# An attention-and-FFN kernel on one core: image lines issued ahead of the queries, key weights on the scalar queue, a third of the first tile's output products an iteration earlier

## The chip, the core and the metric

One NeuronCore of a Trainium2 chip, alone on the chip. The metric is device time of one execution in microseconds; lower is better. Times are medians of single runs, each 1.9 us or so longer than the span from the first to the last instruction that a profile shows. "Before" is the kernel before the change, "the changed kernel" the one after. Faster or slower needs two per cent, which is 21 us here. The "clock" is TensorE's, as a share of full speed.

## The reference, cut to what matters

```python
# q: 4 x 12288 x 128, kv: 4 x 384 x 32 x 128 (an image), w_sr: 128 x 128
kv_pool = kv.reshape(B, H // 4, 4, W // 4, 4, C).mean(axis=(2, 4))   # 4 x 4 pixels to one: 768 keys
k = v = kv_pool.reshape(B, -1, C) @ w_sr
a = softmax(q @ k.T / sqrt(C));  x = a @ v                            # 4 x 12288 rows of 128
gate = maximum(x @ w_gate, 0);   val = x @ w_val                      # 128 -> 1536
return (gate * val) @ w_out                                           # 1536 -> 128
```

## The kernel before

The 49152 rows are 96 tiles of 512. The main loop runs over k. In iteration k TensorE takes, interleaved in twelve steps, the scores of tile k, the attention values of tile k-1, the gate and value products of tile k-3 and the output products of tile k-4. ScalarE does the exponentials and the casts of the value products, VectorE multiplies gate by value. All products go through eight PSUM banks, which every function takes from one pool (`bank`). Before the loop comes a start in which the keys of the first image are made while it is still being loaded: pair 0 (four image lines of 512 KB each, `dh` 0 to 3), then pairs 1 and 2. "The eighth image line" is the last one of pair 1.

```python
    w_sr_f32 = const.tile([128, C], FP32)
    nc.sync.dma_start(w_sr_f32, w_sr)              # key weights, 64 KB
    q_load_plain(0, 1)                             # queries of tile 0: 256 KB in rows of 2 KB
    kv_load(0, 0)                                  # four image lines, 512 KB each, rows of 4 KB
    q_load_plain(1, GRP)                           # queries of tiles 1 to 3: 768 KB
    for pair in range(1, NJC // 2):
        kv_load(0, pair)
...
    idle = bank([128, 128])
    for _ in range(34):                            # warm-up products
        nc.tensor.matmul(idle, ident16, ident16, start=True, stop=True)
...
    q_cast(0)                                      # VectorE: queries to 16 bits
    q_turn_pe(0)                                   # TensorE: transposed, VectorE: copied
    turn_open(0, 0)
    for dh in range(r):                            # TensorE: transposes that add up the lines
        turn_add(0, 0, line(0, dh), first=dh == 0, final=dh == r - 1)
    q_cast(1)
    project(0, 0)
...
    for k in range(LAG, last + 1):                 # LAG = 3; iteration 3 is the first
        ...
        for step in range(NFB):                    # twelve steps
            kO, kF = k - LAG - 1, k - LAG
            if 0 <= kO:
                out_proj(kO, step)                 # four products of 128 columns
                ...
            if kF < NT:
                value_proj(kF, step)               # TensorE 512 columns, ScalarE cast
            if k == LAG:                           # attention values left over from the start
                own, left = left[:2], left[2:]
                for kV, jc, half in own:
                    values(kV, jc, half)
                    if jc == NJC - 1:
                        keep_sums(kV, half)                  # VectorE: reciprocal
                        keep_values(kV, half, nc.scalar)     # ScalarE: two scalings by it
                        if half == 1:
                            x_turn(kV)
            elif step % 2 == 0:
                if k < NT:
                    scores(k, step // 2)           # TensorE 512 columns, ScalarE exponential
            elif k > GRP and k - 1 < NT:           # not in iteration 4
                values(k - 1, 2 * i, half)
                values(k - 1, 2 * i + 1, half)
                ...
            if kF < NT:
                gate_proj(kF, step)                # TensorE 512 columns, VectorE gate * value
```

The softmax here doesn't subtract the row's maximum and nothing guards it: scores larger than these inputs give would overflow.

Of the kernel before, what the change touches and what calls it, by code (L numbers as in the profile page):

```python
# [9 lines left out]
FP32 = mybir.dt.float32  # L10
FP16 = mybir.dt.float16
AF = mybir.ActivationFunctionType
# [4 lines left out]
def kernel(  # L17
# [22 lines left out]
    nc = tc.nc  # L40
# [8 lines left out]
    NFB = D_FF // 128  # L49
# [6 lines left out]
    LAG = GRP - 1  # L56
# [6 lines left out]
    const = ctx.enter_context(tc.tile_pool(name="const", bufs=1))  # L63
# [3 lines left out]
    def bank(shape, dtype=FP32):  # L67
        return psum.tile(shape, dtype, tag="bank", name="bank_ps")
# [4 lines left out]
    def q_load(g):  # L73
        if not 0 <= g < NG:
            return
        b, n0 = divmod(g * GRP * T, N)
        q16 = work.tile([128, GRP * NS, C], FP16, tag="q16", bufs=2)
        nc.gpsimd.dma_start(  # L78
            q16, q[b, n0 : n0 + GRP * T, :].rearrange("(p s) c -> p s c", p=128)
        )  # L80
        q16s[g] = q16

    def q_turn(g):
        if not 0 <= g < NG:
            return
        q16 = q16s.pop(g)
        qT = work.tile([128, GRP * NS, 128], FP16, tag="qT", bufs=3)
        nc.sync.dma_start_transpose(qT, q16.rearrange("p s c -> p (s c)"))
        qTs[g] = qT

    def q_load_plain(i0, i1):
        q32 = work.tile([128, i1 - i0, NS, C], FP32, tag=f"q32_{i0}", bufs=1, name="q32")
        nc.sync.dma_start(  # L93
            q32, q[0, 0 : GRP * T, :].rearrange("(p i s) c -> p i s c", p=128, i=GRP)[:, i0:i1]
        )
        for i in range(i0, i1):
            q32s[i] = q32[:, i - i0]

    def q_cast(i):
        q16 = work.tile([128, NS, C], FP16, tag="q16s", bufs=3, name="q16s")  # L100
        nc.vector.tensor_copy(q16, q32s[i])
        q16s[0, i] = q16

    def q_turn_pe(i):
        q16 = q16s.pop((0, i))
        qt_ps = bank([128, NS, 128], FP16)
        for s in range(NS):
            nc.tensor.transpose(qt_ps[:, s, :], q16[:, s, :], ident16)
        if i == 0:
            qTs[0] = work.tile([128, GRP * NS, 128], FP16, tag="qT", bufs=3, name="qT")  # L110
        nc.vector.tensor_copy(qTs[0][:, i * NS : (i + 1) * NS, :], qt_ps)
# [7 lines left out]
    kv16 = const.tile([128, B, NJC, 2 * C + 4], FP16)  # L119
    kv_in = {}  # L120

    def kv_load(b, pair):
        parts = work.tile([128, r, 2, r, C], FP32, tag="kv_in", bufs=3)
        rows = kv[b, pair * 2 * HC : (pair + 1) * 2 * HC].rearrange(
            "(hp dh) (wp h dw) c -> dh hp wp (h dw c)", dh=r, h=2, dw=r
        )
        for dh in range(r):
            nc.sync.dma_start(parts[:, dh].rearrange("p h dw c -> p (h dw c)"), rows[dh])  # L128
        kv_in[b, pair] = parts

    s3s, kv_Ts, key_banks = {}, {}, {}
# [14 lines left out]
    def turn_open(b, pair):  # L146
        kv_Ts[b, pair] = bank([128, 2, 128])

    def turn_add(b, pair, lines, first=False, final=False, chunks=(0, 1)):

        n = lines.shape[2]
        for h in chunks:
            for i in range(n):
                nc.tensor.matmul(  # L154
                    kv_Ts[b, pair][:, h], lines[:, h, i], ident, is_transpose=True,
                    start=(first and h == i == 0), stop=(final and i == n - 1),
                    skip_group_check=True,
                )
        if final and h == 1:
            kvT = work.tile([128, 2, 128], FP32, tag="kvT", bufs=2)  # L160
            nc.vector.tensor_copy(kvT, kv_Ts[b, pair])  # L161
            kv_Ts[b, pair] = kvT

    def project(b, pair):
        pr = bank([128, 2, 128])
        nc.tensor.matmul(pr, w_sr_f32, kv_Ts.pop((b, pair)), start=True, stop=True)  # L166
        nc.vector.tensor_scalar(  # L167
            kv16[:, b, 2 * pair : 2 * pair + 2, 0:C], pr, 1.0 / (r * r), None, op0=ALU.mult
        )
# [32 lines left out]
    def keep_sums(k, half):  # L202
        rinvs[k, half] = work.tile([128, 2, 1], FP32, tag="rinv", bufs=4, name="rinv")
        nc.vector.reciprocal(rinvs[k, half], x_banks[k, half][:, :, C : C + 1])  # L204
# [49 lines left out]
    def out_add(k, fb, s, o_ps, first):  # L254
        nc.tensor.matmul(  # L255
            o_ps, hTs[k][:, fb, s * 128 : (s + 1) * 128], wo16[:, fb, :],
            start=first, stop=(fb == NFB - 1), skip_group_check=True,
        )

    def out_proj(k, fb):  # L260
        if fb == 0:
            o_banks[k] = bank([128, NS, 128])
        for s in range(NS):
            out_add(k, fb, s, o_banks[k][:, s, :], fb == 0 and s == 0)

    def out_scale(k, engine, own, o_ps=None):
        if k not in o_sbs:
            o_sbs[k] = work.tile([128, NS, 128], FP32, tag="o_sb", bufs=3, name="o_sb")
        o_sb, o_ps = o_sbs[k][:, own], o_ps if o_ps is not None else o_banks[k]
        if engine is nc.scalar:  # L270
            nc.scalar.mul(o_sb, o_ps, 1.0 / X_SCALE**2)
        else:
            nc.vector.tensor_scalar(o_sb, o_ps, 1.0 / X_SCALE**2, None, op0=ALU.mult)  # L273
# [28 lines left out]
    ctx.enter_context(tc.manual_schedule())  # L302


    warm = const.tile([128, 1], FP32)
    nc.vector.memset(warm, 0.0)
    nc.scalar.activation(warm, warm, AF.Exp)
    ident = const.tile([128, 128], FP32)
    make_identity(nc, ident)
    ident16 = const.tile([128, 128], FP16)  # L310
# [1 line left out]
    nc.gpsimd.memset(kv16[:, :, :, 2 * C : 2 * C + 4], 1.0 / X_SCALE)  # L312

    w_sr_f32 = const.tile([128, C], FP32)
    nc.sync.dma_start(w_sr_f32, w_sr)
    q_load_plain(0, 1)
    kv_load(0, 0)
    q_load_plain(1, GRP)
    for pair in range(1, NJC // 2):
        kv_load(0, pair)  # L320

    wg16 = const.tile([128, D_FF], FP16)
    wv16 = const.tile([128, D_FF], FP16)
# [12 lines left out]
    def line(pair, dh):  # L336
        return kv_in[0, pair][:, dh]
# [9 lines left out]

    s2s = {}
    q_cast(0)
    q_turn_pe(0)  # L350
    turn_open(0, 0)
    for dh in range(r):
        turn_add(0, 0, line(0, dh), first=dh == 0, final=dh == r - 1)
    q_cast(1)
    project(0, 0)
    q_cast(2)
# [68 lines left out]
    for k in range(LAG, last + 1):  # L425
        g, ph = divmod(k, GRP)
        if ph == 1:
            q_turn(g + 1)
            q_load(g + 2)
        b = k // NST + 1  # L430
        at = k % NST - (NST - NJC - 6)
        for step in range(NFB):
            kO, kF = k - LAG - 1, k - LAG
            half, i = divmod(step // 2, NJC // 2)
            if 0 <= kO:
                out_proj(kO, step)
                if step == NFB - 1 and k < last:
                    out_scale(kO, nc.vector if kF < NT - 2 else nc.scalar, slice(0, NS))
                    out_store(kO, slice(0, NS))
            if kF < NT:  # L440
                value_proj(kF, step)
            if k == LAG:
# [4 lines that stand above are left out]
                        keep_sums(kV, half)  # L447
                        keep_values(kV, half, nc.scalar)
# [4 lines that stand above are left out]
                    scores(k, step // 2)  # L453
            elif k > GRP and k - 1 < NT:
                values(k - 1, 2 * i, half)
                values(k - 1, 2 * i + 1, half)
                if i == NJC // 2 - 1:
                    keep_sums(k - 1, half)
                    keep_values(k - 1, half)
                    if half == 1:  # L460
                        x_turn(k - 1)
            if kF < NT:
                gate_proj(kF, step)
            if k == LAG and step == 2:
                x_turn_pe(1)
            if b < B:
                if step == 1 and 0 <= at < NJC and at % 2 == 0:
                    kv_load(b, at // 2)
                if step == 3 and 0 <= at - 2 < NJC:
                    pool_pixels(nc.gpsimd, b, (at - 2) // 2, at % 2)  # L470
                pair = (at - 5) // 2
                if at % 2 == 1 and 0 <= pair < NJC // 2:
                    if step == 2:
                        turn_open(b, pair)
                        turn_add(b, pair, s3s.pop((b, pair))[:, :, None], True, True)
                    if step == 4:
                        project(b, pair)
                    if step == 8:
                        turn_values(b, pair)
# [33 lines left out]
```

## Time and profile before

| | before |
|---|---|
| median, first three runs | 1047.56 us (1047.43 to 1047.84) |
| span of the profile | 1046.1 us |
| busy TensorE / VectorE / ScalarE | 99 / 87 / 87 % |
| first value product of iteration 3 | 32.46 us |
| second scores product of iteration 5 | 52.98 us |

The last two rows are marks in the trace. The first says how long the start took. The second lies in the part where TensorE runs without a gap, and from there to the end the kernel takes 993 us or so. What lies between the two, 20.52 us, is the stretch of iterations 3 and 4 with the beginning of 5, and it tells of the output products apart from the loads. The profile's lines for before are in the prediction.

### The profile page before, as it was taken

Reading aid. Unit: us, or ns where it says so; the run is one execution under the profiler, and the core shown is the slowest. Engines: PE = TensorE matmul, PEld = TensorE weight load, DVE = VectorE, ACT = ScalarE, POOL = GpSimd, SP = SyncE. Lnnn points to the kernel's source line nnn. Section 1 sums busy time; section 2 is a strip of 40 time slices with the busy share of each in tenths; the row PEclk is TensorE's granted clock in tenths of the full one; section 3 lists DMA queues with packets and bytes.
Section 4 is the critical chain, followed back from the end, with each engine's and each line's share of the span. In section 5 each row is a group of like instructions: output and inputs, shape, how many; then the busy total and the mean of one; then the engine's idle time right before and its main releaser. Section 6 shows DMA issues by size and latency. Waiting matters only on the chain.

```text
span 1046.1 us, 25977 instructions
## 1 busy us (share of the span) xinstructions
PE 1036.3 (99%) x9984; PEld 691.0 (66%) x9984; DVE 913.6 (87%) x1679; ACT 908.6 (87%) x1741; POOL 107.6 (10%) x127
## 2 busy tenths in 40 slices
PE   8999999999999999999999999999999999999998
PEld 6566666666666666666666666666666666666665
DVE  3788889898888888998888888889988888888898
ACT  3888888888888888888888888888888888888887
POOL 2000045200000015500000003430000000000000
PEclk9999999999999999999999999999999999999999
DMA  8733256241322335523224144551332322212111
GB/s 298 123 81 72 73 186 164 55 87 32 86 52 65 74 122 139 156 60 72 56 63 87 31 87 132 148 151 41 77 62 56 72 64 55 67 32 67 32 47 47
DMA packets 125853, 90.75 MB, mean 87 GB/s; under 512 B 103328, under 2 KB 104224, under 8 KB 125728
## 3 DMA queue, kind: packets, MB, share of 16 engines
q1 hardware_dynamic: 120288, 75.85, 26.9%
q0 software_dynamic: 5440, 13.24, 7.7%
q8 instruction: 78, 1.28, 0.5%
q14 instruction: 47, 0.39, 0.1%
HBM read 52.76 MB, written 25.17 MB: 74 GB/s over the span
## 4 chain that ended last, share of the span: by engine, by line
PE 97%; DMA 1%; SPq 1%; DVE 1%; ACT 0%; issue 0%; DVEq 0%; ACTq 0%
PE bank_ps L255 25%; PE bank_ps L234 24%; PE bank_ps L245 24%; PE bank_ps L196 12%; PE bank_ps L185 12%; DMA parts<-in_kv_dram 1%; PE bank_ps L154 1%; PE bank_ps L166 1%; SPq L128 0%; ACT aT L186 0%; ACT x L210 0%; ACT val L238 0%; SPq L93 0%; PE bank_ps L174 0%; DVE hT L248 0%
## 5 line engine op out<-in xcount | busy, mean ns | idle before, releaser
L248 DVE SCALAR_TENSOR_TENSOR hT<-bank_ps,val 128x512 f16<-128x512 f32 x1152 | 759.6, 687 | 100.7 <-ACT val L238 74.8
L238 ACT CAST val<-bank_ps 128x512 f16<-128x512 f32 x1152 | 677.8, 591 | 112.1 <-PE bank_ps L234 107.8
L255 PEld LDWEIGHTS <-hT 128*128 128x128 f16 x4608 | 351.4, 98 | 199.9 <-issue 0.4
L255 PE MATMUL bank_ps<-wo,hT 128*128 128x128 f16 x4608 | 443.6, 219 | 0.0
L234 PE MATMUL bank_ps<-xT,wv 128*128 128x512 f16 x1152 | 437.1, 379 | 0.1
L245 PE MATMUL bank_ps<-xT,wg 128*128 128x512 f16 x1152 | 436.1, 379 | 0.1
L186 ACT ACTIVATE aT<-bank_ps 128x512 f16<-128x512 f32 x576 | 346.4, 605 | 17.9 <-PE bank_ps L185 17.5
L196 PE MATMUL bank_ps<-kv,aT 128*128 128x129 f16 x2304 | 223.4, 220 | 0.0
L196 PEld LDWEIGHTS <-aT 128*128 128x128 f16 x2304 | 177.2, 98 | 68.3 <-issue 0.4
L185 PE MATMUL bank_ps<-qT,kv 128*128 128x512 f16 x576 | 216.6, 379 | 1.5 <-DVE kv L167 0.8
L245 PEld LDWEIGHTS <-wg 128*128 128x128 f16 x1152 | 111.5, 97 | 66.1 <-issue 1.0
L234 PEld LDWEIGHTS <-wv 128*128 128x128 f16 x1152 | 112.7, 98 | 0.5 <-issue 0.4
L212 DVE TENSOR_TENSOR x<-bank_ps,rinv 128x256 f16<-128x256 f32 x188 | 79.7, 424 | 6.7 <-DVE rinv L204 0.2
L78 POOL DMA_DIRECT2D q<-in_q_dram x23 | 12.5, 543 | 569.7 <-DMA qT<-q 569.5
L273 DVE TENSOR_SCALAR o_sb<-bank_ps 128x512 f32<-128x512 f32 (+1 forms) x95 | 64.0, 674 | 1.3 <-PE bank_ps L255 1.3
L137 POOL TENSOR_TENSOR s<-parts 128x512 f32<-128x512 f32 x36 | 45.2, 1267 | 163.9 <-DMA parts<-in_kv_dram 122.4
L185 PEld LDWEIGHTS <-kv 128*128 128x128 f16 x576 | 55.8, 98 | 2.5 <-DVE kv L167 1.6
L204 DVE RECIPROCAL rinv<-bank_ps 128x2 f32<-128x2 f32 x192 | 30.7, 160 | 1.6 <-PE bank_ps L196 1.6
L139 POOL TENSOR_TENSOR s<-s 128x512 f32<-128x512 f32 x18 | 22.8, 1268 | 1.4
L141 POOL TENSOR_TENSOR c<-s 128x256 f32<-128x256 f32 x18 | 13.0, 725 | 1.4
L161 DVE COPY kvT<-bank_ps 128x256 f32<-128x256 f32 x12 | 5.0, 417 | 7.8 <-PE bank_ps L154 7.8
L144 POOL TENSOR_TENSOR kv_s<-c 128x128 f32<-128x128 f32 x18 | 8.2, 454 | 1.4
(37 smaller groups left out, 82.5 us busy)
## 6 DMA issues: line engine op xcount, KB each, us to landing
parts<-in_kv_dram SPq DMA_DIRECT2D x48, 512.0 KB, 6.1
out_dram<-o_sb SPq DMA_DIRECT2D x95, 256.0 KB, 2.1
q<-in_q_dram POOLq DMA_DIRECT2D x23, 512.0 KB, 5.3
xT<-x SPq DMA_TRANSPOSE x94, 2.5
q<-in_q_dram SPq DMA_DIRECT2D x1, 768.0 KB, 8.5
wv<-in_moe_w_val_dram POOLq DMA_DIRECT2D x2, 192.0 KB, 4.4
wg<-in_moe_w_gate_dram POOLq DMA_DIRECT2D x2, 192.0 KB, 4.8
wo<-in_moe_w_out_dram POOLq DMA_DIRECT2D x1, 384.0 KB, 9.6
```

The costliest lines, as they stand in the source:

```text
L137: eng.tensor_tensor(s2[:, i], parts[:, 2 * i, h], parts[:, 2 * i + 1, h], op=ALU.add)
L185: nc.tensor.matmul(s_ps, kv16[:, k // NST, jc, 0:C], qT_of(k), start=True, stop=True)
L186: nc.scalar.activation(aTs[k][:, jc, :], s_ps, AF.Exp, scale=qk_scale)
L196: nc.tensor.matmul(x_ps[:, i, :], aTs[k][:, jc, s * 128 : (s + 1) * 128], kv16[:, k // NST, jc, C : 2 * C + 1], start=(jc == 0 and i == 0) ...
L204: nc.vector.reciprocal(rinvs[k, half], x_banks[k, half][:, :, C : C + 1])
L212: nc.vector.tensor_tensor(x16s[k][:, 2 * half : 2 * half + 2, :], x_ps[:, :, 0:C], rinv.to_broadcast([128, 2, C]), op=ALU.mult,)
L234: nc.tensor.matmul(va_ps, wv16[:, fb * 128 : (fb + 1) * 128], xTs[k], start=True, stop=True)
L238: nc.scalar.copy(val, va_ps)
L245: nc.tensor.matmul(g_ps, wg16[:, fb * 128 : (fb + 1) * 128], xTs[k], start=True, stop=True)
L248: nc.vector.scalar_tensor_tensor(hTs[k][:, fb, :], g_ps, 0.0, vals.pop((k, fb)), op0=ALU.max, op1=ALU.mult)
L255: nc.tensor.matmul(o_ps, hTs[k][:, fb, s * 128 : (s + 1) * 128], wo16[:, fb, :], start=first, stop=(fb == NFB - 1), skip_group_check=True,)
L273: nc.vector.tensor_scalar(o_sb, o_ps, 1.0 / X_SCALE**2, None, op0=ALU.mult)
```

## The change

The intent, not yet a finding: image lines reach the chip earlier, because nothing stands ahead of them in SyncE's queue; the array's clock comes up earlier, because the first transposes follow the warm-ups at once; and TensorE fills its stalls at the end of iteration 3 with work that iteration 4 would have to do.

```diff
--- before.py
+++ after.py
@@ -119,13 +119,15 @@
     kv16 = const.tile([128, B, NJC, 2 * C + 4], FP16)
     kv_in = {}
 
-    def kv_load(b, pair):
+    def kv_load(b, pair, between=None):
         parts = work.tile([128, r, 2, r, C], FP32, tag="kv_in", bufs=3)
         rows = kv[b, pair * 2 * HC : (pair + 1) * 2 * HC].rearrange(
             "(hp dh) (wp h dw) c -> dh hp wp (h dw c)", dh=r, h=2, dw=r
         )
         for dh in range(r):
             nc.sync.dma_start(parts[:, dh].rearrange("p h dw c -> p (h dw c)"), rows[dh])
+            if dh == 1 and between is not None:
+                between()
         kv_in[b, pair] = parts
 
     s3s, kv_Ts, key_banks = {}, {}, {}
@@ -302,9 +304,6 @@
     ctx.enter_context(tc.manual_schedule())
 
 
-    warm = const.tile([128, 1], FP32)
-    nc.vector.memset(warm, 0.0)
-    nc.scalar.activation(warm, warm, AF.Exp)
     ident = const.tile([128, 128], FP32)
     make_identity(nc, ident)
     ident16 = const.tile([128, 128], FP16)
@@ -312,12 +311,15 @@
     nc.gpsimd.memset(kv16[:, :, :, 2 * C : 2 * C + 4], 1.0 / X_SCALE)
 
     w_sr_f32 = const.tile([128, C], FP32)
-    nc.sync.dma_start(w_sr_f32, w_sr)
-    q_load_plain(0, 1)
-    kv_load(0, 0)
+    nc.scalar.dma_start(w_sr_f32, w_sr)
+    kv_load(0, 0, between=lambda: q_load_plain(0, 1))
     q_load_plain(1, GRP)
     for pair in range(1, NJC // 2):
         kv_load(0, pair)
+
+    warm = const.tile([128, 1], FP32)
+    nc.vector.memset(warm, 0.0)
+    nc.scalar.activation(warm, warm, AF.Exp)
 
     wg16 = const.tile([128, D_FF], FP16)
     wv16 = const.tile([128, D_FF], FP16)
@@ -347,10 +349,11 @@
 
     s2s = {}
     q_cast(0)
-    q_turn_pe(0)
     turn_open(0, 0)
     for dh in range(r):
         turn_add(0, 0, line(0, dh), first=dh == 0, final=dh == r - 1)
+        if dh == 1:
+            q_turn_pe(0)
     q_cast(1)
     project(0, 0)
     q_cast(2)
@@ -432,8 +435,13 @@
         for step in range(NFB):
             kO, kF = k - LAG - 1, k - LAG
             half, i = divmod(step // 2, NJC // 2)
+            if k == LAG and step >= NFB - 4:
+                out_proj(kF, step - NFB + 4)
+            if k == LAG + 1 and step % 3 > 0:
+                out_proj(kO, 4 + step - 1 - step // 3)
             if 0 <= kO:
-                out_proj(kO, step)
+                if kO > 0:
+                    out_proj(kO, step)
                 if step == NFB - 1 and k < last:
                     out_scale(kO, nc.vector if kF < NT - 2 else nc.scalar, slice(0, NS))
                     out_store(kO, slice(0, NS))
```

## The prediction

> **What bounds the kernel now.** I read the page's first part, then its chain of work that ended last.
>
> ```profile
> PE 1036.3 (99%) x9984; PEld 691.0 (66%) x9984; DVE 913.6 (87%) x1679; ACT 908.6 (87%) x1741; POOL 107.6 (10%) x127
> PE 97%; DMA 1%; SPq 1%; DVE 1%; ACT 0%; issue 0%; DVEq 0%; ACTq 0%
> ```
>
> A busy PE may only be a pipelined one, so the second line decides: 97% of the chain is TensorE's own work. In order of time, the chain is one unbroken row of matmuls from 43 us to the end. So there is no gain in the body; whatever moves the moment at which TensorE runs without gaps moves the end by as much. The change touches only what lies before 52 us. I therefore read that stretch closely, first the chain in order of time (start, length, what):
>
> ```profile
> 0.74 0.40 SPq L315
> 1.20 0.42 SPq L93
> 1.67 0.65 SPq L128
> ...
> 7.02 10.92 DMA parts<-in_kv_dram
> 18.04 0.70 DVE kv_s L343
> ```
>
> The end hangs on the landing at 17.94 us of the eighth image line (the last of pair 1). The waits of pair 0 and of the first query are not on the chain. The lines ahead of it are SyncE's issues: the key weights, the first queries, then image lines. How fast bytes come in is told by the table of stretches (us; then busy time per engine, clock, DMA share, GB/s):
>
> ```profile
> 0.00:2.00 2.00, 0.28 (x3) 0.29 (x4) 0.06 (x1) 1.27 (x1) 1.11 (x8) 1.00 0.04 13
> 2.00:3.00 1.00, 1.00 (x13) 1.00 (x11) 0.00 (x0) 0.22 (x2) 0.00 (x0) 1.00 0.64 156
> 3.00:4.00 1.00, 1.00 (x12) 1.00 (x11) 0.00 (x0) 0.00 (x0) 0.00 (x0) 1.00 0.79 127
> 4.00:5.00 1.00, 1.00 (x13) 1.00 (x11) 0.07 (x1) 0.00 (x0) 0.00 (x0) 1.00 0.76 309
> 13.00:20.00 7.00, 6.02 (x51) 3.87 (x51) 4.97 (x11) 4.04 (x8) 0.00 (x0) 1.00 1.03 414
> ```
>
> From 13 us the queue is full at 414 GB/s, but between 2 and 4 us it moved 0.28 MB in 2 us, while 64 KB of key weights and 256 KB of the first queries stood at its head. Next, iterations 3 and 4 (32.5 to 41 and 41 to 51 us), in the timeline by engine (start, length, engine, line):
>
> ```profile
> 38.12 0.38 PE L234 MATMUL bank_ps<-xT,wv 128*128 128x512 f16 x1
> 38.77 0.38 PE L234 MATMUL bank_ps<-xT,wv 128*128 128x512 f16 x1
> 39.66 0.38 PE L234 MATMUL bank_ps<-xT,wv 128*128 128x512 f16 x1
> 40.41 0.38 PE L234 MATMUL bank_ps<-xT,wv 128*128 128x512 f16 x1
> 41.98 0.38 PE L185 MATMUL bank_ps<-qT,kv 128*128 128x512 f16 x1 [0.36 <-ACT x L210]
> 44.68 0.39 PE L255 MATMUL bank_ps<-wo,hT 128*128 128x128 f16 x4
> 44.90 0.38 PE L234 MATMUL bank_ps<-xT,wv 128*128 128x512 f16 x1
> 46.43 0.38 PE L234 MATMUL bank_ps<-xT,wv 128*128 128x512 f16 x1
> 44.67 0.67 ACT L186 ACTIVATE aT<-bank_ps 128x512 f16<-128x512 f32 x1
> 46.10 0.71 ACT L186 ACTIVATE aT<-bank_ps 128x512 f16<-128x512 f32 x1
> ```
>
> To be seen: in the last steps of iteration 3 the value products start 0.65, 0.89 and 0.75 us apart, where the work between them is only 0.65, 0.65 and 0.44 us (0.22 per 512-column product or group of four 128-column products, from 44.68 to 44.90). TensorE stalls there. In iteration 4 it takes 1.53 us for two steps (44.90 to 46.43), and ScalarE, two casts and an exponential, 1.43 us (44.67 to 46.10): nearly level.
>
> **What the Trainium skill says.** "DMA: Bandwidth & Descriptors", section "Issuing engines are not separate DMA queues", says that issuing from several engines saves only the sequencer's issue time. Here that is 0.40 us for the key weights, plus 0.42 us for the queries that now come later; the first image line's issue can start at 0.74 instead of 1.67 us. "TensorE: Matmul & The Clock Gate", section "What's actually happening", gives about 3.4 us of sustained work before the array goes from half clock to full. The trace agrees in kind: 34 warm-up products take 3.81 us in all, about 0.11 each, and those of the body 0.056; the page's clock row, at 1.00, doesn't show it. "PSUM — Partial Sum Buffer", section "Specifications (TRN2)", gives eight banks; the wait at 41.98 us, for a ScalarE read of an attention bank, fits a TensorE that has run ahead until no bank is free. "ScalarE: Activation LUTs", section "What ACT_TABLE_LOAD costs", gives 1283 ns, and the trace 1.28 us.
>
> **The change part by part.**
>
> *Loads.* The bytes up to the eighth image line stay the same: 64 + 256 + 768 + 8 x 512 KB = 5.31 MB, which is 12.8 us at 414 GB/s. It landed at 17.94, so 5.1 us are start-up. About 1.8 us of that is issue and latency (no bytes to speak of in the first 2 us) and stays. By 7 us the stretches have 1.36 MB (0.03 + 0.16 + 0.13 + 0.31 + 0.37 + 0.38, the last two from the rows for 5 to 7 us); at about 400 GB/s from 1.8 us on it would be 2.08. The missing 0.72 MB are 1.8 us. That is the most the new order can win back. It puts two 512 KB loads of 4 KB pieces at the head, where there were 512-byte and 2 KB pieces, so that the slow first microseconds carry more bytes. Yet part of the slowness may belong to the first microseconds themselves or to the queries' rows wherever they stand. I take a little over half: 1.0 us earlier for all later landings, with 0.2 to 1.8 possible. It reaches the chain whole: the lines behind stay in a full queue, and what follows 18.04 (add, transposes, copy, projection, scores) is dependent work of unchanged length.
>
> *Key weights on the scalar queue.* They're wanted by the first projection at 12.79 us and land within a few us: nothing beyond the issue time counted above.
>
> *Table load behind the issue.* ScalarE does its 1.28 us load some 0.5 us later, and its first exponential is at 14.44 us: nothing.
>
> *Query transposes behind the second line.* Four transposes with a cast ahead move from 5.41 us to a gap between lines. TensorE transposed pair 0 from 7.01 to 12.28 us without a gap, the first five in 1.33 us and the last twelve in 1.47: at first it ran at half clock, after an idle 0.98 us. With the first line landing about when the warm-ups end (near 5.4 us), that gap closes. Pair 0 so ends at least 1 us earlier too and doesn't become the bound; it had slack anyway (VectorE idled 1.09 us before 18.04).
>
> *Output products.* Four of the first tile's twelve groups, 4 x 0.22 = 0.88 us, go from iteration 4 into steps 8 to 11 of iteration 3, and the eight left spread over iteration 4, two in every three steps. In iteration 3 there is room: stalls of 0.24 and 0.31 us in the steps shown, then up to step 1 of iteration 4 (42.63) some 0.8 us more. Their inputs, the first four gated blocks, are ready near 37 us, the output weights at 35. In iteration 4 TensorE's work falls from 6 x 1.53 = 9.2 to 8.3 us, but ScalarE's stays at 6 x 1.43 = 8.6: it becomes the bound. The gain isn't 0.88 but about 9.2 - 8.6 = 0.6, as ScalarE is still behind at the start and stays so to the end; the banks bound how far TensorE can be ahead. The lag from scores to exponential was 1.26 us at 41.98 (exponential at 43.24) and 0.68 at 51.22 (51.90). If it stays near 1.2, that is again 0.55. From iteration 5 TensorE needs 1.75 us for two steps with the value products, ScalarE still 1.43, so the lag is worked off without cost. I take 0.55, with 0.2 to 0.8 possible.
>
> Sum: 1047.56 - 1.0 - 0.55 = 1046.0 us.
>
> **The rivals.**
>
> 1. *The load start is slow whatever comes first.* Then only issue time is gained and the image lines meet the same slow microseconds: 0.2 to 0.3 us. For it: the first image line, with packets of 4 KB, came 2.1 us after the first queries (4.93 to 7.01), not in the 1.27 us that 512 KB take at 414 GB/s. Against it: by 5 us the rate was 365 GB/s and more. With the products' 0.55: 1046.7.
> 2. *ScalarE takes all of the moved work back.* If the eight banks let TensorE be no further ahead at the end of iteration 4 than now (one output bank is held longer, and iteration 5 holds an attention bank too), it waits there for what it saved. For it: the stall at 41.98 is just such a wait. Against it: in iteration 4 as it is, TensorE ran 1.26 to 0.68 us ahead without stalling after 43 us. The gain is then the loads' alone: 1046.5.
> 3. *The moved products lengthen iteration 3.* They stand in TensorE's order ahead of value products that ScalarE needs. ScalarE lagged by about 1.7 us there (step 8's product at 38.12, its cast in the group that begins at 39.28), more than the 0.88 inserted; I give this little. It would cost at most 0.5: 1047.
> 4. *Everything works:* 1.8 + 0.8 us: 1045.0.
>
> **Range and chances.** Single runs of before lie 0.4 us apart, so changes of this size are measurable, but two per cent would be 21 us, more than the 8 us or so of TensorE's gaps in the whole program. Nothing in the change adds work or a long wait. Faster by over 2%: 0.005; within 2%: 0.99; slower by over 2%: 0.005. The range is rival 4's and, at the upper end, rivals 1 and 2 together (1047.3): 1044.9 to 1047.2.
>
> **What would show it.** In the changed kernel's chain the last image line of pair 1 should land near 16.9 us (17.7 under rival 1), the first image transposes start before 6 us, and TensorE's first value product of iteration 3 come at 31.4 instead of 32.46 us. The rate from 2 to 4 us should exceed 200 GB/s. In iteration 4 the exponentials should still be 1.43 us apart without idle time on ScalarE, the lag from scores to exponential above 1 us, and TensorE show small stalls. From the first value product of iteration 3 to that of iteration 5 (32.46 to 51.01, 18.55 us) it should take 18.0. It would be wrong if the body showed new waits: 10.5 us per tile is assumed untouched, and 0.02 us on each of the 92 would outweigh everything above. It would also be wrong if the bank rotation, which now gives out one bank earlier, made a later product wait.

## The result, and the profile after

The changed kernel took 1048.12 us (median of 6 runs, 1047.35 to 1050.02), before 1047.76 (6 runs, 1047.43 to 1048.98). The ratio is 1.0005, with a 95% interval from 0.9992 to 1.0017. Ratios are the mean time of one kernel's fast runs over that of the other's of the same rounds, so not quite the ratio of these medians. "The same" was right as a class, but 1048.12 lies outside the range of 1044.9 to 1047.2: the 1.55 us that I predicted are not there.

The profile of one run hides this at first. Its span is 1045.5 against 1046.1 us, and the chain is what it was:

```profile
PE 97%; DMA 1%; SPq 1%; DVE 0%; ACT 0%; issue 0%; DVEq 0%
```

In order of time, the chain of the changed kernel begins (start, length, what):

```profile
0.74 0.66 SPq L128
1.46 0.58 SPq L128
...
6.57 10.82 DMA parts<-in_kv_dram
17.49 0.70 DVE kv_s L345
```

The first line is issued at 0.74 as expected, and the eighth landed at 17.39 us, not at 16.9: 0.55 earlier than in before's profile. The table of stretches of the changed kernel (columns as in the prediction) says why it is no more:

```profile
2.00:3.00 1.00, 1.00 (x13) 1.00 (x11) 0.00 (x0) 0.63 (x2) 0.00 (x0) 1.00 0.95 146
3.00:4.00 1.00, 1.00 (x12) 1.00 (x11) 0.00 (x0) 0.00 (x0) 0.00 (x0) 1.00 0.86 319
5.00:6.00 1.00, 1.00 (x9) 1.00 (x8) 0.00 (x0) 0.00 (x0) 0.00 (x0) 1.00 0.90 330
6.00:7.00 1.00, 1.00 (x7) 1.00 (x6) 0.00 (x0) 0.00 (x0) 0.00 (x0) 1.00 0.82 221
```

From 2 to 4 us the rate is up, 0.47 MB against 0.28. But it falls to 330 and 221 GB/s just when the queries are in the queue; in before those stretches had 365 and 381. The slow stretch has moved to where the queries now are.

In iterations 3 and 4 the products moved as the diff says, and the stretch between the two marks, 31.91 to 52.34, is 20.43 us against 20.52. So the move gained 0.09 us and not 0.55. In the timeline, TensorE's scores (L187) at the end of iteration 4 and in iteration 5, then ScalarE's exponentials (L188) of the same three products:

```profile
48.77 0.38 PE L187 MATMUL bank_ps<-qT,kv 128*128 128x512 f16 x1
50.46 0.38 PE L187 MATMUL bank_ps<-qT,kv 128*128 128x512 f16 x1
52.34 0.38 PE L187 MATMUL bank_ps<-qT,kv 128*128 128x512 f16 x1
49.85 0.82 ACT L188 ACTIVATE aT<-bank_ps 128x512 f16<-128x512 f32 x1
51.29 0.85 ACT L188 ACTIVATE aT<-bank_ps 128x512 f16<-128x512 f32 x1
53.02 0.60 ACT L188 ACTIVATE aT<-bank_ps 128x512 f16<-128x512 f32 x1
```

The lag from product to exponential is 1.08, 0.83 and 0.68 us. TensorE had its lead in iteration 4, and lost it within the first three steps of iteration 5: there it took 1.69 and 1.88 us for pairs of steps that took 1.52 and 1.76 in before (49.70 to 51.22 to 52.98). ScalarE's pace of 1.43 us for two steps is the same in both kernels all through iteration 4.

So far it is 0.55 from loads and 0.09 from products, and the profile's span agrees. The median doesn't. Of the six runs, two took 1050.02 and 1049.55 us, with a mean clock of 0.997, the others 1.000. The experiments had three questions: is the loads' half microsecond real, what ate the products' gain, and what are the slow runs? "Slow run" is my own name for some that took 2 us or more longer than the fastest of their kernel.

### The profile page after: what moved, and what is told of

It reads as the page before. It is cut to its first block, busy times and chain, and to the rows that moved or that the text cites. A ratio compares the mean times of both kernels' runs of the same rounds, so it can differ in the third digit from the quotient of the medians.

```text
span 1045.5 us, 25976 instructions
## 1 busy us (share of the span) xinstructions
PE 1036.0 (99%) x9984; PEld 690.1 (66%) x9984; DVE 913.3 (87%) x1679; ACT 908.9 (87%) x1741; POOL 107.8 (10%) x127
## 4 chain that ended last, share of the span: by engine, by line
PE 97%; DMA 1%; SPq 1%; DVE 0%; ACT 0%; issue 0%; DVEq 0%
PE bank_ps L257 25%; PE bank_ps L247 24%; PE bank_ps L236 24%; PE bank_ps L198 12%; PE bank_ps L187 12%; DMA parts<-in_kv_dram 1%; PE bank_ps L156 1%; PE bank_ps L168 1%; SPq L128 0%; ACT aT L188 0%; SPq L93 0%; PE bank_ps L176 0%; DVE kv L169 0%; DVE kvT L163 0%; PE bank_ps L229 0%
## 5 line engine op out<-in xcount | busy, mean ns | idle before, releaser
L188 ACT ACTIVATE aT<-bank_ps 128x512 f16<-128x512 f32 x576 | 346.0, 604 | 16.9 <-PE bank_ps L187 16.6
L187 PE MATMUL bank_ps<-qT,kv 128*128 128x512 f16 x576 | 216.4, 379 | 1.1 <-DVE kv L169 0.5
L187 PEld LDWEIGHTS <-kv 128*128 128x128 f16 x576 | 55.8, 98 | 2.4 <-DVE kv L169 1.4
```

The lines of the kernel that those rows point to most:

```text
L187: nc.tensor.matmul(s_ps, kv16[:, k // NST, jc, 0:C], qT_of(k), start=True, stop=True)
L188: nc.scalar.activation(aTs[k][:, jc, :], s_ps, AF.Exp, scale=qk_scale)
```

## The experiments

Before and the changed kernel first ran in six rounds, each experiment in five (two of them gave four runs). The columns "landing" (of the eighth image line) and "stretch" (first value product of iteration 3 to the second scores of iteration 5) are from the one trace of each kernel.

| kernel | median us (range) | before, same rounds | ratio, 95% interval | landing us | stretch us |
|---|---|---|---|---|---|
| before | 1047.76 (1047.43 to 1048.98) | | | 17.94 | 20.52 |
| changed kernel | 1048.12 (1047.35 to 1050.02) | 1047.76 | 1.0005, 0.9992 to 1.0017 | 17.39 | 20.43 |
| e1 loads only | 1047.96 (1047.25 to 1049.73) | 1047.90 | 1.0002, 0.9990 to 1.0015 | 17.75 | 20.50 |
| e2 products only | 1047.91 (1047.60 to 1048.49) | 1047.90 | 1.0000, 0.9987 to 1.0012 | 17.47 | 20.42 |
| e3 changed kernel again | 1047.88 (1047.42 to 1050.06) | 1047.90 | 1.0006, 0.9994 to 1.0019 | 17.82 | 20.42 |
| e4 changed, late scaling | 1047.14 (1047.04 to 1047.46) | 1047.90 | 0.9993, 0.9980 to 1.0007 | 17.95 | 19.44 |
| e5 new loads, old products, late scaling | 1047.24 (1046.14 to 1048.66) | 1047.90 | 0.9995, 0.9982 to 1.0008 | 18.65 | 19.04 |
| e6 changed, whole queries | 1047.97 (1047.49 to 1048.11) | 1047.90 | 1.0000, 0.9987 to 1.0012 | 17.08 | 20.43 |
| e7 changed, fillers | 1048.52 (1048.26 to 1048.74) | 1047.90 | 1.0006, 0.9992 to 1.0019 | 18.29 | 20.43 |
| e8 changed, few warm-ups | 1047.94 (1047.39 to 1049.20) | 1047.90 | 1.0002, 0.9990 to 1.0015 | 18.61 | 20.43 |
| e9 before, late scaling | 1046.21 (1045.98 to 1046.82) | 1047.93 | 0.9985, 0.9971 to 0.9999 | 17.47 | 19.03 |
| e10 e9 with products moved | 1046.94 (1046.66 to 1047.62) | 1047.93 | 0.9992, 0.9979 to 1.0004 | 18.33 | 19.45 |
| e11 e9, key weights on scalar queue | 1046.34 (1046.17 to 1046.65) | 1047.93 | 0.9985, 0.9971 to 0.9999 | 17.64 | 19.04 |
| e12 whole queries, reordered, late scaling | 1050.10 (1049.87 to 1051.13) | 1047.93 | 1.0023, 1.0009 to 1.0036 | 17.18 | 19.04 |

All outputs are right.

### The parts alone: e1, e2, e3

e1 is the changed kernel with the old output products:

```diff
-            if k == LAG and step >= NFB - 4:
-                out_proj(kF, step - NFB + 4)
-            if k == LAG + 1 and step % 3 > 0:
-                out_proj(kO, 4 + step - 1 - step // 3)
             if 0 <= kO:
-                if kO > 0:
-                    out_proj(kO, step)
+                out_proj(kO, step)
```

> Only the new order of the loads (with the key weights on the scalar queue and the later query transposes); output products as before. Theory (loads give 0.55 us, moved products 0.1): the first value product of iteration 3 at about 31.9 us against 32.46 before and 31.91 in the changed kernel, the second scores product of iteration 5 at about 52.4 (before 52.98, changed 52.34), span about 1045.5. Rival (the loads' gain in the changed kernel was luck of one run): first value product anywhere from 31.5 to 32.5, no nearer to the changed kernel than to the one before. The time itself lies within 0.1 per cent of before in either case.

e2 is before with just these lines the other way round.

> Only the output products moved; loads as before. Theory: ScalarE sets the pace of iteration 4 and the banks don't let TensorE carry its lead into iteration 5, so the gain from the first value product of iteration 3 to the second scores product of iteration 5 (20.52 us before) is about 0.1: 20.4 us; lag from scores to exponential about 1.05 us through iteration 4 and 0.68 from the second scores of iteration 5 on. The prediction's term, 0.55, would make it 20.0 us.

e3 is the changed kernel, unedited.

> The changed kernel again, beside its parts and the kernel before on one chip. Theory: span 0.5 to 0.7 us below before's in the profile; the time, whose single runs scatter by about 1 us, between 1.2 us below and 0.3 us above. Rival (the change costs something in the body that the one profile didn't show): time at least 0.3 us above before, as in the first six runs (1048.12 against 1047.76).

Half of my theory fell. The products' part held: 20.42 us with the products moved (e2, e3), 20.50 without (e1). The loads' part didn't. e1's first value product came at 32.27 and e3's at 32.34, where I had expected about 31.9, and e2, with the *old* load order, had it at 31.99 and its eighth line at 17.47. That is what my rival said: the 0.55 us were the luck of one run. Over all traces here the old order of image lines and queries landed its eighth line at 17.94, 17.47, 17.47, 17.64 and 18.33 us (before, e2, e9, e11, e10), the new one with the first queries between the lines at 17.39, 17.75, 17.82, 17.95, 18.65, 18.29 and 18.61. The means are 17.8 and 18.1. The landing scatters by a microsecond from run to run, and if the new order does anything to it, it isn't a gain. In the seven traces of the new order the second line landed between 6.16 and 6.38 us, but the first queries between 7.60 and 8.88, and the eighth line 9.65 to 10.14 after them: most of the scatter arises while the queries are loaded. What follows the landing doesn't scatter: in nine traces (before, the changed kernel, e1 to e4, e7, e8, e9) the first value product comes 14.52 or 14.53 us after it (14.67 in e11 and 14.70 in e10). e3's span, 1045.9, missed its theory too (0.5 to 0.7 below before's 1046.1).

The slow runs were there again: one of five in e1 (1049.73), two of five in e3 (1050.06 and 1050.02), none in e2 and none among the nine of before.

### What ate the products' gain: e4, e5, e9, e10

In iteration 3 of the changed kernel ScalarE waits for VectorE's reciprocals before each pair of scalings but the first:

```profile
38.22 0.63 ACT L212 ACTIVATE x<-bank_ps,rinv 128x128 f16<-128x128 f32 x2 [0.46 <-DVE rinv L206]
40.76 0.63 ACT L212 ACTIVATE x<-bank_ps,rinv 128x128 f16<-128x128 f32 x2 [0.46 <-DVE rinv L206]
```

The chain of before goes through these two engines at the end of iteration 3, and not through TensorE's own work (start, length, what; extracts):

```profile
36.24 0.63 ACT x L210 x2
...
37.98 0.40 DVE hT L248
39.28 0.59 ACT val L238
...
41.57 0.37 ACT x L210
```

A reciprocal stands in VectorE's order behind the gated block of the step before, which in turn waits for ScalarE's cast of that step; the two engines wait for each other, and TensorE, run ahead until no bank is free, for both. e4 lets each pair of scalings come a step later, behind another cast, so that the reciprocal is ready:

```diff
+                if due and due[0] == step:
+                    keep_values(*due[1:], nc.scalar)
+                    if due[2] == 1:
+                        x_turn(due[1])
                 own, left = left[:2], left[2:]
                 for kV, jc, half in own:
                     values(kV, jc, half)
                     if jc == NJC - 1:
                         keep_sums(kV, half)
-                        keep_values(kV, half, nc.scalar)
-                        if half == 1:
-                            x_turn(kV)
+                        due = (step + 1, kV, half)
```

> The changed kernel, but in iteration 3 each pair of ScalarE scalings of the attention values comes one step later, behind the next value cast, so that ScalarE doesn't idle for the reciprocal (0.57, 0.46, 0.46 us in the changed kernel, one ahead of each pair after the first). Theory (ScalarE's backlog at the start of iteration 4 is what ate the moved products' gain): ScalarE reaches its first exponential of iteration 4 1.0 to 1.5 us earlier than 42.69, TensorE stalls less around 38 to 43 us, and the second scores product of iteration 5 comes 0.5 to 1.0 us earlier than 52.34; span 1044.5 to 1045.0. Rival (the banks alone set it: the attention bank is now held a step longer): no gain or a loss of up to 0.3 us.

The stretch fell from 20.43 to 19.44, within the theory's 0.5 to 1.0, and all five runs were below all nine of before. The idle time for reciprocals is gone. In absolute time the numbers of the expectation weren't met in full (first exponential of iteration 4 at 42.31 instead of 41.2 to 41.7, second scores of iteration 5 at 51.92, 0.42 earlier), since this run's start was 0.57 later than the changed kernel's; counted from the first value product, the exponential came 0.95 earlier.

e5 is the same with the output products back in iteration 4.

> The late scaling of the run before this one, but the output products all in iteration 4, as in the kernel before. From the first value product of iteration 3 to the second scores of iteration 5: 20.52 us in before, 20.43 with the products moved, 19.44 with products moved and late scaling. Theory (ScalarE is what TensorE waits for, so moved products pay only where ScalarE has room): with late scaling alone TensorE becomes the bound of iteration 4, and it is 19.7 to 20.0 us, so that the move of the products is worth 0.3 to 0.5 us there. Rival (the products' move is worth 0.1 whatever ScalarE does): 19.5.

It was neither: 19.04 us, better than with the products moved. This trace was of a run with a slow start, though (below), so I repeated the pair on the old loads. e9 is before with the late scaling alone, e10 is e9 with the moved products of e2.

> The kernel before with the late scaling of iteration 3 alone: old loads, output products all in iteration 4. With the changed loads this form took 19.04 us from the first value product of iteration 3 to the second scores of iteration 5 (before: 20.52), but after a start with a half clock. Theory (ScalarE's idle time for the reciprocals is what TensorE waits for in iterations 3 and 4, and the old load order has no long gap for the clock to fall back in): 19.1 to 19.4 us, time 0.9 to 1.4 us below before in all five runs, none 1.5 us above its fellows. Rival (19.04 came from the late start, which gave ScalarE time to catch up): 19.5 us or more, time no more than 0.8 below before.

> The run before this one with the four groups of output products moved into iteration 3 as in the change. Theory: with ScalarE no longer waiting, the groups stand in TensorE's order ahead of value products that ScalarE now needs, so they cost: about 19.45 us for the same stretch, as in the late scaling on the changed kernel (19.44), and 0.2 to 0.5 us more time than the run before this one. The prediction's idea (the move fills stalls) would make it 0.3 us less instead.

Both came out on the theory's side, the sizes only in part: 19.03 us, a little under the 19.1 to 19.4 expected, and 19.45; in time 1046.21, 1.72 below before where 0.9 to 1.4 was expected, and 1046.94, 0.73 more where 0.2 to 0.5 was (of that 0.73 the stretch explains 0.42; the rest may be the landing, 17.47 in one trace and 18.33 in the other, which isn't shown). So the same move gains 0.09 us where ScalarE is behind and costs 0.42 where it isn't. ScalarE in e10, around the end of iteration 3 (start, length, engine, line, idle time before and who ended it):

```profile
39.31 1.32 ACT L238 CAST val<-bank_ps 128x512 f16<-128x512 f32 x2
40.93 0.59 ACT L238 CAST val<-bank_ps 128x512 f16<-128x512 f32 x1 [0.30 <-PE bank_ps L234]
41.41 0.63 ACT L210 ACTIVATE x<-bank_ps,rinv 128x128 f16<-128x128 f32 x2
```

and in e9:

```profile
38.28 1.60 ACT L238 CAST val<-bank_ps 128x512 f16<-128x512 f32 x3
39.76 0.65 ACT L210 ACTIVATE x<-bank_ps,rinv 128x128 f16<-128x128 f32 x2
40.27 1.10 ACT L238 CAST val<-bank_ps 128x512 f16<-128x512 f32 x2
```

In e10 ScalarE idles 0.30 us for a value product that stands behind the moved groups in TensorE's order; in e9 it never waits there. That is the rival 3 of the prediction, to which I gave little. It needs a ScalarE that keeps up, and in the changed kernel it doesn't.

e9's stretch of 19.03 us is just TensorE's own work. A 512-column product and a group of four narrow ones take it the same time, seven of them 1.53 us in iteration 4, or 0.2186 each. Iteration 3 has 24 value and gate products, ten groups of attention values and one of transposes; iteration 4 has 24 value and gate products, 12 groups of output products and 6 scores; and ten more come before the second scores of iteration 5. That is 87, or 19.0 us. Its chain holds nothing but TensorE from 31.25 us on.

### The loads: e6, e11

e6 loads all queries at once, in rows of 8 KB, behind the four lines of pair 0:

```diff
-    kv_load(0, 0, between=lambda: q_load_plain(0, 1))
-    q_load_plain(1, GRP)
+    kv_load(0, 0)
+    q_load_plain(0, GRP)
...
-    q_cast(0)
     turn_open(0, 0)
     for dh in range(r):
         turn_add(0, 0, line(0, dh), first=dh == 0, final=dh == r - 1)
-        if dh == 1:
-            q_turn_pe(0)
-    q_cast(1)
     project(0, 0)
+    q_cast(0)
+    q_turn_pe(0)
+    q_cast(1)
```

> The changed kernel, but all four query tiles come as one load of 8 KB rows behind the four lines of pair 0, and their transposes behind the projection. In the profiles so far the 256 KB of the first queries (2 KB rows) and the two image lines behind took from 6.2 to about 10.4 us, 1 to 1.4 us more than 768 KB at 412 GB/s, and at the head of the queue they were as slow. Theory (the 2 KB rows are slow wherever they stand): the eighth image line lands at 16.4 to 16.9 us instead of 17.4 to 17.95, and the first value product of iteration 3 comes 0.6 to 1.2 us earlier than the 31.9 to 32.5 seen with the other orders. Rival (the loss belongs to the first microseconds, whichever load is there): landing between 17.3 and 18.0 as always.

The landing improved to 17.08, less than the 16.4 to 16.9 expected and better than anything with the first queries apart. From the second to the third line's landing, 512 KB took 1.88 us instead of 1.27, and with no queries between them; the queries' 1 MB then took 2.47, full rate. With the queries between the lines, the same two landings were 2.93 to 4.01 us apart in seven traces, for 768 KB that would take 1.91 at 412 GB/s. So both hold a part: the rows of 2 KB cost 0.4 us or more of their own (2.93 less 1.88 is 1.05, and at full rate they'd take 0.64), and the first eight microseconds are slow with any load. How the two divide isn't settled. The time gained nothing, as the first value product came at 32.62: by the trace's chain, VectorE's work on the later queries held pair 1's first addition up until 15.83 us, and its addition for pair 2 (19.97 to 21.61) stood ahead of the copy of pair 1's keys.

e11 is e9 with the key weights on the scalar queue.

```diff
-    nc.sync.dma_start(w_sr_f32, w_sr)
+    nc.scalar.dma_start(w_sr_f32, w_sr)
```

> The kernel before with late scaling and only the key weights' load moved to the scalar queue, so that the first queries are at the head of SyncE's queue. If issue time counted, all landings would come 0.4 us earlier: eighth image line at 17.1 to 17.5 us against 17.47 and 17.94 in the two traces of the old order. Theory (the first microseconds are slow and scatter by half a microsecond whatever the issue): 17.4 to 18.0, time equal to the late scaling alone within 0.3 us.

The first line was issued 0.47 us earlier (1.20 instead of 1.67) and the eighth landed at 17.64, within the scatter; the time, 1046.34, is e9's 1046.21 within noise. An earlier issue on SyncE brought nothing here; one trace alone couldn't show it, but the times of four and five runs should show 0.4 us.

### The slow runs: e7, e8, and the traces of e5 and e12

e7's edit puts 14, 10, 4 and 8 warm-up products behind line 1, the query transposes, line 2 and line 3:

```diff
+        fill((0, 14, 4, 8)[dh])
         if dh == 1:
             q_turn_pe(0)
+            fill(10)
```

> The changed kernel with 36 more idle products between the image lines of pair 0, so that TensorE has no long gap between 5 and 12 us. In the changed kernel and the one with its loads alone 5 of 16 timed runs took about 2 us more (1049.6 to 1050.1, mean clock 0.997 where known), in the kernel before and the one with its products alone none of 20. Theory (in those runs the clock falls back or stays low because TensorE waits for lines between 7 and 12 us): none of five runs above 1049. Rival (chance, or a cause elsewhere): one or two of five above 1049.

e8 has `range(10)` for `range(34)` in the warm-up.

> The changed kernel with 10 warm-up products instead of 34, so TensorE is idle from about 2.8 us to the first line at 5. Theory as in the run with fillers: the clock comes up later or falls back more often, at least two of five runs 1.5 to 3 us longer than the others, and a trace of such a run shows transposes 0.21 us apart beyond 12 us. Rival: no more slow runs than with 34.

e7 had no slow run, as the theory says (at the rate of 7 in 31 given below, five runs would have none about once in four times), but all five were at 1048.3 to 1048.7. Its trace has the eighth line at 18.29 and nothing else out of place; why five runs should all be so I can't say. e8 missed: one run 1.8 us above its fastest and one 1.3. The traced one was that of 1048.7, with a late landing (18.61) and the clock at full from 9.02 us on by its clock record (the transposes are 0.21 us apart up to 8.42, 0.11 from 10.38). Both late runs of e8 have a mean clock of 1.000. So these two don't decide.

The decision came from a run that happened to be traced. e5's profiled run was one of its two slow ones (1048.66 and 1048.51; the fastest took 1046.14), with a mean clock of 0.996. Its stretches (us, busy times, then clock, DMA share, GB/s):

```profile
5.00:8.00 3.00, 2.28 (x18) 1.72 (x16) 0.00 (x0) 0.00 (x0) 0.00 (x0) 1.00 0.96 294
8.00:11.00 3.00, 1.00 (x10) 0.83 (x10) 0.85 (x2) 0.00 (x0) 0.00 (x0) 1.00 1.02 421
11.00:14.00 3.00, 2.51 (x13) 1.82 (x11) 0.32 (x1) 0.00 (x0) 0.00 (x0) 0.55 1.00 411
14.00:18.00 4.00, 3.75 (x19) 2.51 (x20) 2.55 (x8) 1.08 (x2) 0.00 (x0) 0.50 1.03 414
18.00:22.00 4.00, 3.69 (x31) 2.66 (x30) 2.80 (x5) 3.04 (x6) 0.64 (x1) 0.98 0.92 365
```

and the reason, in its timeline:

```profile
9.39 0.40 PE L108 MATMUL bank_ps<-ident,q16s 128*128 128x128 f16 x4 [1.91 <-DVE q16s L101]
10.40 3.25 PE L156 MATMUL bank_ps<-ident,parts 128*128 128x128 f32 x16 [0.61 <-DMA parts<-in_kv_dram]
```

The third number from the right, the clock, drops to 0.55 and 0.50. By the clock record of the trace it was halved from 11.31 to 18.13 us. TensorE had come to full clock, done the first two lines by 7.5 us, and then waited for the queries, whose transposes stand ahead of lines 2 and 3, until 9.39, and for line 2 until 10.40. In 3 us it had 1.00 us of work. Then the clock fell, and everything up to 18.13, the first scores among it, ran at half speed: the first value product of iteration 3 came at 34.57. With this run's landing (18.65) it would have been 33.17 at the usual 14.52 us, so 1.40 us go with the clock and the rest of the delay is the late landing. The long gap goes with the new order: the first two lines are done early, and then TensorE waits in one piece for the queries, which landed here at 8.88, the latest of the seven traces. An earlier rise of the clock isn't part of it: by the clock records the first rise came at 4.63 to 10.24 us in the five traces of the old order and at 4.48 to 9.02 in the seven of the new.

e12 confirms it without wanting to:

```diff
+    for jc in range(2):
+        scores(0, jc)
+    turn_values(0, 0)
     q_cast(1)
     q_turn_pe(1)
+    for jc in range(2):
+        scores(1, jc)
+    q_cast(2)
+    q_cast(3)
+    turn_open(0, 1)
+    turn_add(0, 1, add_lines(1, 0, nc.vector), first=True)
     for i in range(2, GRP):
         q_turn_pe(i)
```

(with project(0, 1) ahead of pair 2's additions, the loads of e6, late scaling and old products).

> Late scaling and old products, with all queries in one load of 8 KB rows behind pair 0's lines, and VectorE's work reordered so that pair 0 doesn't hold pair 1 up: first scores straight behind the first query's transposes, the first addition of pair 1 ahead of the last two query copies, the projection of pair 1 ahead of pair 2's additions. Theory (the earlier landing of the eighth line, 17.08 us in the other run of that load, was lost on VectorE's pair 0 work): first value product of iteration 3 at 31.3 to 31.8 us, span 0.3 to 0.9 below the late scaling on the old loads. Rival (pair 0 stays the bound): 32.3 or later and no gain.

The theory failed wholly: first value product at 36.44, all four runs near 1050. The eighth line landed at 17.18, in time. But TensorE had little to do for longer, 3.21 us of work between 10.7 and 17.8 us:

```profile
12.00:16.00 4.00, 1.50 (x12) 0.85 (x13) 2.22 (x7) 1.08 (x2) 0.00 (x0) 0.98 1.03 420
16.00:20.00 4.00, 3.19 (x14) 2.22 (x14) 1.77 (x3) 1.08 (x2) 0.10 (x1) 0.50 1.02 411
20.00:23.00 3.00, 2.91 (x20) 1.63 (x18) 2.06 (x4) 1.65 (x4) 3.00 (x5) 0.56 0.54 138
```

1.50 us of work in 4, and the clock is at half from 15.82 to 22.65 us. Here the order makes the gap in the one trace I have, and all four runs are slow alike, with mean clocks of 0.995 to 0.997.

Why only some runs? The clock records of the 14 traces tell more. Every stretch at full clock lasted a whole number of steps of 3.413 us (2 in e5 up to 11.31, 3 in e12 up to 15.82, 301 to 305 in those that ended with the program). The last step before each of these 16 falls held at most 1.50 us of TensorE work (1.31 in e5, 1.50 in e12, at most 1.42 at the ends); no other step at full clock held less than 1.75. The same gap lying across two steps is harmless: e6 had only 1.19 us of work in the 3.41 from 10.55 us and kept its clock, as that was split between steps with 1.96 and 2.50. And the steps lie differently in every run, as the first rise shows. So the order makes the gap, and where the steps happen to lie decides whether it counts. That is read from the traces; no run was made to test it.

Over all runs, counting as slow what is 2 us or more above the fastest run of its kernel: with the first queries between the lines and no fillers (changed kernel, e1, e3, e4, e5, e8) 7 of 31; with the old order of queries and lines (before, e2, e9, e10, e11) none of 44. If chance alone put the seven, all of them falling among 31 of the 75 would happen about once in 750 cases (the limit of 2 us was set after the runs). The mean clock draws the same line without that limit: all seven have 0.996 to 0.998, the other 24 have 0.999 or 1.000, and so have the 38 runs of the old order whose clock is on record. For one of the seven the trace shows the clock's fall in the gap; for the other six the mean tells that it was at half for some microseconds, not where. (e6 has two runs with 0.998 as well, at 1048.10 and 1048.11, some 0.6 us above its fastest.)

## Why the prediction was wrong

- **"I take a little over half: 1.0 us earlier for all later landings".** This step failed. I took the slow microseconds from 2 to 4 us as a cost of what stood at the head of the queue. The new order moved the slow stretch to where the queries now stand, from 5 to 9 us, and lost there what it had gained; by e6 a part of it is there with any load. The measured gain is none that stands out of a scatter of 1 us in the landing (means 17.8 for the old order, 18.1 for the new). The scatter itself I didn't foresee: I read the landing from one trace and treated it as a property of the kernel. That the lines behind and the work after the landing follow it unchanged was right (14.52 us).
- **"I take 0.55, with 0.2 to 0.8 possible"**, for the output products. The mechanism was right up to its last link, which failed. There was room in iteration 3 (with the four groups and without, the first scores of iteration 4 come 9.52 us after the first value product). ScalarE did become the bound of iteration 4, at 1.43 us for two steps, and TensorE did run ahead, with lags of 1.05 to 1.26 us. But "from iteration 5 ... the lag is worked off without cost" was false: TensorE stalled in the first steps of iteration 5 until its lag was 0.68, and with that gave back most of what it had gained: 0.24 us up to the first value product of iteration 5 (18.31 us where 18.0 was predicted and before had 18.55), 0.09 at its second scores. This was rival 2, down to its reason that more banks are held in iteration 5; the reason itself I haven't tested, only the stall. What I missed in before was the reason of the stalls at the end of iteration 3: its chain runs through ScalarE and VectorE there, from 36.24 to 41.94 us, and I read only its start and the unbroken matmuls from 43 us on. Filling TensorE's gaps left ScalarE where it was (its first exponential of iteration 4 comes 10.78 us after the first value product in both kernels); taking ScalarE's waits away gave 1.49 us (20.52 to 19.03, e9).
- **"What follows 18.04 ... is dependent work of unchanged length"; "nothing in the change adds ... a long wait".** Not so in some runs. Clearing the way for the first two lines made a gap behind them, and 7 of 31 runs of such kernels took 2 us or more longer than the fastest, all with a lower mean clock; the one traced had its clock halved for 6.8 us, which goes with 1.40 us of its delay. Without its two slow runs the changed kernel's first six have a median of 1047.79, against 1047.76. The early full clock that I had counted on isn't there either: before's own trace rose at 10.24 us, the changed kernel's at 6.85, but over all traces the two orders overlap.
- **Right:** no effect anywhere near two per cent, an untouched body, the key weights and the table load free of cost, the first image transposes before 6 us (5.33), a rate above 200 GB/s from 2 to 4 us, exponentials 1.43 apart in iteration 4 without idle time.
- **The range.** Rivals 1 and 2, which I named for its upper end, add up to 1047.3, but the range ends at 1047.2, and either way a time equal to before's lay outside it. The sum started from 1047.56, the median of three runs, where six gave 1047.76.

Predicted were -1.0 and -0.55; measured are about 0 and -0.09, and something on average for the slow runs (7 of 31, some 2.1 us above the mean of their fellows, or 0.5). That adds up to about +0.4; the means of the first six runs differ by +0.5 (1048.47 and 1047.99), the medians by +0.36. With runs that scatter like these I make no more of it than that the signs agree.

The version that beats both is e9, the kernel before with the late scaling: 1046.21 us against 1047.93, ratio 0.9985 (0.9971 to 0.9999), every run below every run of before. It takes away what TensorE waited for in iteration 3 instead of filling the wait.

## What to carry to other kernels

Filling an engine's stall with later work gains only what the engine it waits for has to spare; ask first why that one is late, and here taking each pair of scalings a step later gave 1.5 us where the filler gave 0.09. A load that is slow at the head of a queue may be slow anywhere, and the landing in one trace is one draw: take three before building on half a microsecond. An earlier start of a part isn't free when it leaves a gap behind in which the array's clock can fall, and a trace in which it didn't fall doesn't clear the gap: in the next run the steps lie elsewhere.

## What the Trainium skill lacked or had wrong

- "TensorE: Matmul & The Clock Gate", section "What's actually happening", has the clock fall "after ≥1 idle window (~3.4µs)". Here it fell though TensorE wasn't idle for a whole window: in e5 it had 1.00 us of work between 8 and 11 us and worked on up to the fall at 11.31, in e12 1.50 us between 12 and 16. The page gives no threshold of work in a window (a later section speaks of frequent short idles, without a number): here the clock fell after steps of 3.41 us with 1.50 us of work or less and never after one with 1.75 or more. The half clock then lasted 6.83 us in both, twice the page's window.
- "DMA: Bandwidth & Descriptors", section "Bandwidth", gives rates by the size of a transfer. It has nothing on a kernel's first microseconds: between 2 and 4 us the queue moved 127 to 156 GB/s with key weights and 2 KB query rows at its head, and 146 to 319 with 4 KB rows, against 414 later; and the landing of the eighth line scattered between 17.39 and 18.65 us with the same bytes.
- No page that I read says how far TensorE can run ahead of the engines that read its banks; here its lag was 1.26 us at most in iteration 4 and 0.68 from the third step of iteration 5 on.
